# Ten head pairs' scores from scaled float16 halves, and more of the feed-forward's evacuations on ScalarE

## The chip, the cores and the metric

The kernel runs on one NeuronCore of a Trainium2 chip. The metric is the device time of one execution in microseconds (us); "before" is the median of three runs. Five engines work side by side: TensorE (PE), VectorE (DVE), ScalarE (ACT), GpSimd (POOL) and SyncE (SP), which issues the transfers.

## What is computed

```python
scores = scale * q @ k.T                       # 4 batches x 8 heads, 576 x 576, depth 64
thresh = max(scores, axis=-1) - tau
scores = where(scores >= thresh, scores, -1e9)
attn   = softmax(scores)                       # sum + 1e-9 in the denominator
x = (attn @ v) as [2304 tokens, 512]
g = relu(x @ w_in) ** 2                        # 512 -> 2048
x = g @ w_out                                  # 2048 -> 512
logits = x @ phi                               # 32 slots: 8 experts x 4
d = softmax(logits, over tokens); slots = d.T @ x
slots = per expert: relu(slots @ w1) @ w2      # 512 -> 1024 -> 512
out = softmax(logits, over slots) @ slots
```

## The kernel before

**Order.** A planner inside the kernel (class `Plan`) places every operation. `add(kind, engine, cost, fn, deps, key, takes, ...)` registers one with a planned duration, a key (lower goes first) and the buffers that it takes; on each engine the planner starts the ready operation with the lowest key. The result is a fixed order on every engine, SP's queue included. The costs are the planner's; no time here comes from them.

**Attention.** A pair is two heads of one batch; there are 16 pairs in 20 jobs (the first four pairs are cut into two jobs each). A job walks over tiles of 128 queries: j = 0 to 3 hold 128 queries of each of the two heads, j = 4 is the mixed tile with the last 64 queries of both. A full job has five tiles, and the 20 jobs have 80. For each tile:

- `s_mm` on PE: scores in float32, line 555 for the 64 remaining keys of both heads at once, line 560 for 512 keys of one head (64 rows of the array each); the mixed tile has lines 549 and 552.
- `top` on DVE (line 576): the scores, scaled, into `u`, and their row minimum; `bound` on POOL (582); `expo` on ACT (588); `keep` on DVE (592): the mask and the row sum.
- then, for all but the first batch, `high` on ACT (610) and `low` on POOL (614) split the result into float16 halves `hl`; `dturn` lets a DMA transpose them (621, SP); `av_split` multiplies by v's halves in float16 (713, 718). Mixed tiles and the first batch transpose on PE (line 250) and multiply in float32 (705). `evac` on DVE writes the feed-forward's input `xp` (735).

v's halves are made by `split_v`: squares with a running sum (480), the sum over partitions on PE (486), a power of two from it on DVE (`power`, 274 to 278), the high half on ACT (514), the low half on DVE (518).

**Feed-forward.** A unit is 256 tokens; there are nine. Two of a batch can begin once its four pairs are done, and `rem` holds the remainders of all batches. A unit has 16 blocks of 12 float16 matmuls on PE (998, "FFN blocks" below); after each two, `relu` (1007) on ACT and `square` on ACT (1015), or on DVE (1013) where `m2 % 4` is in `SQD`. Then comes its post work: logits (813 to 826), eight groups of four transposes (250), an evacuation of each group, on ACT (910) or on DVE (912) where `j` is in `GKD`, and the sums over tokens (925). PE fills the gaps of the next batch's attention with these.

**Loads.** `raw64` is a set of eight 512 KB buffers: first for the weights' conversion, later for `w_pre`, loads of weights for the mixture at the end.

Of the kernel before, what the change touches and what calls it, by code (L numbers as in the profile page):

```python
# [9 lines left out]
F32 = mybir.dt.float32  # L10
# [131 lines left out]
def tile_kernel(  # L142
# [139 lines left out]
    def conv_ops():  # L282
# [124 lines left out]
        for n in range(RB):  # L407
            add("w_pre", "SP", 0.5, lambda: state["wr"](), stores, 300.0 + n, ["raw64"], dma=1.46)

    xp, ev_at, xs_op, att = {}, {}, {}, []  # L410

    def attn_ops():
# [27 lines left out]
        def prep(x):  # L440
# [10 lines left out]
            for nm in "kqv":  # L451
                def lraw(nm=nm):
                    if nm == "v":
                        t = raw[p, nm] = at.tile([128, 2, 4 * D], F32, tag=nm + "raw", name="raw", bufs=2)
                        nc.sync.dma_start(
                            out=t, in_=v[b, h0:h0 + 2, 0:512, :].rearrange("h (r j) d -> r h (j d)", j=4)
                        )
                        return
                    t = d[nm + "t"] = at.tile([128, SQ], F32, tag=nm + "t", name=nm + "t", bufs=QKB)
                    nc.sync.dma_start(out=t, in_=src[nm][b, n])  # L460
                ld[nm] = add("lraw", "SP", 0.6, lraw, [], k0 - (5 if nm != "v" else 2), [nm + ("raw" if nm == "v" else "t")],
                             dma=0.73 if nm == "v" else 0.95)
# [3 lines left out]
            split = any(by_dma(x, j // 2) for j in jobs[x][1] if j < 4)  # L466
            if split or 0 in jobs[x][1]:
                split_v(x, split)

        def split_v(x, split):  # L470
# [12 lines left out]
            def stats():  # L483
                d["ps"] = mm_tile()
                for i in range(2):
                    nc.tensor.matmul(
                        d["ps"][:, 0:1], ones.to_broadcast([128, 128]), d["mx"][:, i:i + 1], start=i == 0, stop=i == 1
                    )

            def scales():  # L490
                mx = d["mx"]
                e = mx[:, 4:5]
                nc.vector.tensor_scalar(e, d["ps"][:, 0:1], 2.0**-80, None, ALU.max)
                if n == 0:
# [24 lines left out]

            ab = add("v_abs", "ACT", 0.9, absum, [d["v_op"], d["vr_op"]], k0, ["mx", "vh"])  # L520
            st = add("v_sum", "PE", 0.4, stats, [ab], k0, ["mm"])
            sc = add("v_scale", "DVE", 0.9 if split else 0.3, scales, [st], k0, rel=[("mm", st)])
            if n == NP - 1:
# [7 lines left out]
            plan.release(d["vs_ready"], [("vraw", d["v_op"]), ("vbd", d["vr_op"])])  # L531

        def tiles(p):
            d = P[p]
            b, kk = jobs[p][0] // NP, jobs[p][0] % NP
            G = [dict() for _ in range(3)]
            s_ops, av_ops, m_ops = [], [], []

            def tile_ops(n, j):
# [5 lines left out]
                def s_mm():  # L545
                    s = ps.tile([128, 3, 512], F32, tag="s", name="s", bufs=1)
                    o["s"] = s.rearrange("p c s -> p (c s)")
                    if mixed:
# [9 lines left out]
                    for a in range(2):  # L558
                        i = slice(64 * a, 64 * a + 64)
                        nc.tensor.matmul(s[:, 2 * a], lt[i], d["kt"][i, 0:512], start=True, stop=True)  # L560

                first_g = "first" not in gd
                S_ = add("s", "PE", 1.4, s_mm, d["ready"], k, ["s"])
                s_ops.append(S_)
                heads = (0,) if mixed else (0, 1)
                ks = []
                for a in heads:
# [3 lines left out]
                    def top(a=a, c=c):  # L571
                        if "sm" not in gd:
# [3 lines left out]
                        nc.vector.tensor_scalar(  # L576
                            u, o["s"][:, s0:s0 + S], nscale, None, ALU.mult, ALU.min, accum_out=gd["sm"][:, c:c + 1]
                        )
# [16 lines left out]

                    X = add("top", "DVE", 0.89, top, [S_], k, ["u"] + (["sm"] if first_g and not a else []), [("s", S_)])
                    if first_g and not a:
                        gd["first"] = X
# [182 lines left out]
            for o in s_ops:  # L781
                plan.release(o, [("kt", d["k_op"]), ("qt", d["q_op"])])
            for o in av_ops:
# [9 lines left out]
    def ffn_ops(units):  # L793
# [158 lines left out]
        for n, u in enumerate(units):  # L952
# [7 lines left out]
            def xhi(kk, u=u, x=x, up=up):  # L960
                if kk == 0:
                    x["x"] = xr if u == "rem" else xp[u]
                    x["h"] = fx.tile([128, KC, NU], F16, tag="xh", name="xh", bufs=2)
                nc.vector.tensor_scalar(x["h"][:, kk, :], x["x"][:, kk, :], up, None, ALU.mult)

# [8 lines left out]
            for kk in range(KC):  # L974
                xd = xdeps[kk::KC] + (hs[-1:] if kk else prev.get("hs", [])[-1:] + [xs_op[B if u == "rem" else u[0]]])
                h = add("xhi", "DVE", 0.2, lambda f=xhi, kk=kk: f(kk), xd, HI, [] if kk else ["xh"])
                l = add("xlo", "DVE", 0.37, lambda f=xlo, kk=kk: f(kk), [h] + ls[:1],
# [335 lines left out]
```

## Time and profile before

| | |
|---|---|
| median of three runs | 679.88 us (678.04 to 680.73) |
| the profiled execution | 685.74 us |
| its span | 684.0 us |
| PE, DVE, ACT, POOL busy | 619.8, 471.6, 418.0, 253.6 us |
| mean granted clock of TensorE, of full speed | 0.947 |

The span is the time from the first to the last instruction of the profiled execution. A busy share is an average over stages, so the rows below cut the span.

### The profile page before, as it was taken

The page shows a single profiled execution, that of the slowest core. Times are in us where ns is not written, and L with a number is a line of the kernel's source. Part 1 is how long each engine was busy: PE and PEld are TensorE (multiplying, and loading weights), DVE is VectorE, ACT ScalarE, POOL GpSimd, SP SyncE. Part 2 cuts the span into 40 slices and gives each one's busy share as a digit, 9 for nine tenths or more (in the row PEclk, how much of TensorE's full clock was granted, in tenths as well). Part 3 has the DMA queues.
Part 4 walks back from the last instruction along what each step waited for, and adds up shares of the span by engine and source line. Part 5 has one row for each costly group of instructions (what it writes and reads, how often), then busy time and mean ns, then how long its engine had stood idle before and what let it go on. Part 6 is the DMA issues. An engine that isn't in the chain of part 4 may idle for free.

```text
span 684.0 us, 13526 instructions
## 1 busy us (share of the span) xinstructions
PE 619.8 (91%) x5054; PEld 421.2 (62%) x5054; DVE 471.6 (69%) x1284; ACT 418.0 (61%) x782; POOL 253.6 (37%) x316
## 2 busy tenths in 40 slices
PE   1875989999999999799999999989999999998883
PEld 0443566667776676567757676756776878773321
DVE  4888889967678978887887888878895232231503
ACT  6898976765475776667776667856663443440203
POOL 2765563326434454445654425544550000001000
PEclk9996779997799999999999999989999999999997
DMA  8965154536669475464655627455434940258977
GB/s 279 349 218 174 57 188 163 177 96 180 160 154 257 92 143 106 97 132 86 133 104 116 143 52 138 91 124 89 86 71 134 410 169 33 97 203 308 371 284 276
DMA packets 151281, 111.82 MB, mean 163 GB/s; under 512 B 118960, under 2 KB 124080, under 8 KB 151216
## 3 DMA queue, kind: packets, MB, share of 16 engines
q1 hardware_dynamic: 151216, 110.96, 58.1%
q8 instruction: 40, 0.66, 0.4%
q14 instruction: 25, 0.20, 0.1%
HBM read 73.72 MB, written 8.91 MB: 121 GB/s over the span
## 4 chain that ended last, share of the span: by engine, by line
PE 67%; DVE 14%; ACT 10%; DMA 4%; issue 3%; SPq 1%; POOL 0%; DVEq 0%; ACTq 0%
PE mm L998 26%; PE mm L250 9%; PE s L560 8%; PE po L713 4%; PE po L705 3%; DVE e L592 3%; ACT raw L309 3%; PE mm L925 3%; PE s L555 2%; PE mm L1135 2%; DVE u L576 2%; ACT e L588 2%; DMA w<-in_moe_w_dram 2%; PE s L549 2%; DVE xl L969 2%
## 5 line engine op out<-in xcount | busy, mean ns | idle before, releaser
L998 PEld LDWEIGHTS <-w 128*128 128x128 f16 x1728 | 167.9, 99 | 39.3 <-issue 19.4
L614 POOL TENSOR_TENSOR hl<-e,hl 128x576 f16<-128x576 f32 x96 | 126.3, 1328 | 105.0 <-ACT hl L610 91.4
L998 PE MATMUL mm<-xh,w 128*128 128x256 f16 x1152 | 151.1, 275 | 1.4 <-DVE gk L912 1.3
L592 DVE SCALAR_TENSOR_TENSOR e<-u,sm,e 128x576 f32<-128x576 f32 x144 | 127.1, 898 | 24.8 <-ACT e L588 19.1
L588 ACT ACTIVATE e<-u,sm 128x576 f32<-128x576 f32 x144 | 109.5, 769 | 51.2 <-DVE u L576 47.1
L576 DVE TENSOR_SCALAR_CACHE_REDUCE u<-s,nscale 128x576 f32<-128x576 f32 x144 | 114.8, 811 | 22.7 <-PE s L560 14.7
L582 POOL TENSOR_SCALAR sm<-sm,tau_p 128x1 f32<-128x1 f32 x144 | 63.0, 440 | 124.1 <-DVE u L576 111.2
L998 PE MATMUL mm<-xl,w 128*128 128x256 f16 x576 | 86.9, 274 | 0.0
L1007 ACT ACTIVATE gt<-mm,scl 128x512 f32<-128x512 f32 x72 | 49.1, 682 | 56.0 <-PE mm L998 55.8
L560 PE MATMUL s<-kt,qt 64*128 64x512 f32 x256 | 82.1, 722 | 0.0
L610 ACT ACTIVATE hl<-e 128x576 f16<-128x576 f32 x96 | 63.9, 676 | 19.7 <-DVE e L592 19.3
L555 PE MATMUL s<-kt,qt 128*128 128x128 f32 x128 | 30.0, 319 | 33.2 <-DMA qt<-in_q_dram 13.3
L555 PEld LDWEIGHTS s<-kt,qt 128*128 128x128 f32 x128 | 21.5, 210 | 39.0 <-issue 18.2
L309 ACT ACTIVATE raw<-raw 128x512 f16<-128x512 bf16 x32 | 41.8, 1354 | 5.1 <-DMA raw<-in_moe_w_in_dram 4.3
L250 PE MATMUL mm<-ident_r,e 128*128 128x128 f32 (+1 forms) x224 | 38.8, 311 | 4.7 <-DVE e L592 4.5
L1098 POOL MEMSET cv<- 128x512 f32 x4 | 1.9, 525 | 103.8 <-PE mm L925 103.8
L250 PE MATMUL mm<-ident_r,gt 128*128 128x128 f32 x288 | 39.9, 284 | 0.1
L250 PEld LDWEIGHTS mm<-ident_r,gt 128*128 128x128 f32 x288 | 32.6, 146 | 12.0 <-issue 9.7
L250 PEld LDWEIGHTS mm<-ident_r,e 128*128 128x128 f32 (+1 forms) x224 | 29.7, 161 | 16.5 <-DVE e L592 7.7
L657 ACT ACTIVATE pt<-mm 128x512 f32<-128x512 f32 x48 | 28.3, 601 | 17.3 <-PE mm L250 17.0
L1013 DVE SCALAR_TENSOR_TENSOR gt<-mm,scl,gt 128x512 f32<-128x512 f32 x18 | 13.5, 748 | 33.0 <-ACT gt L1007 32.8
L713 PE MATMUL po<-pt,vh 128*64 128x256 f16 x576 | 35.9, 274 | 0.0
(172 smaller groups left out, 940.2 us busy)
## 6 DMA issues: line engine op xcount, KB each, us to landing
w<-in_moe_w_dram SPq DMA_DIRECT2D x17, 1024.0 KB, 13.1
w<-in_moe_w_dram SPq DMA_DIRECT2D x26, 512.0 KB, 7.9
raw<-in_moe_w_in_dram SPq DMA_DIRECT2D x16, 511.8 KB, 6.8
raw<-in_moe_w_out_dram SPq DMA_DIRECT2D x16, 511.8 KB, 4.4
kt<-in_k_dram SPq DMA_DIRECT2D x20, 320.0 KB, 3.8
qt<-in_q_dram SPq DMA_DIRECT2D x20, 320.0 KB, 4.3
raw<-in_v_dram SPq DMA_DIRECT2D x20, 256.0 KB, 3.5
w_out<-cv SPq DMA_DIRECT2D x16, 256.0 KB, 4.2
```

The costliest lines, as they stand in the source:

```text
L250: nc.tensor.transpose(out_, in_, ident[:n, :n])
L309: nc.scalar.activation(x[:, :, 3].bitcast(F16), x[:, :, 2].bitcast(BF16), AF.Copy)
L555: nc.tensor.matmul(s[:, 1].rearrange("p (c s) -> p c s", s=64)[:, 0:8:7], lt, d["kt"][:, 512:SQ], start=True, stop=True)
L560: nc.tensor.matmul(s[:, 2 * a], lt[i], d["kt"][i, 0:512], start=True, stop=True)
L576: nc.vector.tensor_scalar(u, o["s"][:, s0:s0 + S], nscale, None, ALU.mult, ALU.min, accum_out=gd["sm"][:, c:c + 1])
L582: nc.gpsimd.tensor_scalar(sm[:, 4 + c:5 + c], sm[:, c:c + 1], tau_p, None, ALU.add)
L588: nc.scalar.activation(e, o["u", a], AF.Exp, scale=-1.0, bias=gd["sm"][:, c:c + 1])
L592: nc.vector.scalar_tensor_tensor(e, o["u", a], sm[:, 4 + c:5 + c], e, ALU.is_le, ALU.mult, accum_out=sm[:, 8 + c:9 + c])
L610: nc.scalar.activation(o["hl"][:, a * S:(a + 1) * S], o["e"][:, a * S:(a + 1) * S], AF.Copy)
L614: nc.gpsimd.tensor_tensor(o["hl"][:, (2 + a) * S:(3 + a) * S], o["e"][:, c], o["hl"][:, c], ALU.subtract)
L713: nc.tensor.matmul(po[64 * a:64 * a + 64, :n_], d["vh"][:, y, c0:c0 + D], gd["pt"][:, :, c + 5 * a + m, :], start=i == 0 and m == 0, stop= ...
L998: nc.tensor.matmul(o["h"][:, i * NU:(i + 1) * NU], a, c, start=n_ == 0, stop=n_ == len(terms) - 1)
```

## The change

Jobs 10 to 19 (`QF = 10`, the last ten pairs) no longer use q and k in float32. `lraw` loads them into `raw64`, `split_qk` sums their squares (ACT, PE), makes a power of two for each (DVE), the high halves (ACT) and the low halves (DVE), and six copies from SBUF to SBUF (SP) lay them out so that one matmul over 128 rows multiplies high and low half of q by the high half of k. `fine_mm` adds the high half of q times the low half of k: eight float16 matmuls a tile, four of 512 and four of 64 columns. `GKD` and `SQD` are empty: all squares and all evacuations of transposed groups run on ACT. v's two sums become one matmul of two columns with a reduce on DVE. `w_pre` has a later key. The `XHA` branch is not taken.

```diff
-    GKD = (1, 3)
-    SQD = (3,)
+    GKD = ()
+    SQD = ()
     LOD = (0, 4)
+    QF = 10
+    XHA = ()
+    QL = 16.0
+    LL = 16.0
...
-            add("w_pre", "SP", 0.5, lambda: state["wr"](), stores, 300.0 + n, ["raw64"], dma=1.46)
+            add("w_pre", "SP", 0.5, lambda: state["wr"](), stores, 1000.0 + n, ["raw64"], dma=1.46)
...
+                    if x < QF:
+                        t = d[nm + "t"] = at.tile([128, SQ], F32, tag=nm + "t", name=nm + "t", bufs=QKB)
+                    else:
+                        d[nm + "r"] = t = rows.tile([128, 2 * CW], F32, tag="raw64", name="raw64", bufs=RB)
+                        t = t[:, 0:SQ]
...
-                for i in range(2):
-                    nc.tensor.matmul(
-                        d["ps"][:, 0:1], ones.to_broadcast([128, 128]), d["mx"][:, i:i + 1], start=i == 0, stop=i == 1
-                    )
+                nc.tensor.matmul(d["ps"][:, 0:2], ones.to_broadcast([128, 128]), d["mx"][:, 0:2], start=True, stop=True)
...
+                nc.vector.tensor_reduce(e, d["ps"][:, 0:2], AX.X, ALU.add)
...
+        def split_qk(x):
...
+                nc.scalar.activation(
+                    d[nm + "h"].bitcast(BF16)[:, 1], d[nm + "r"][:, 0:SQ], AF.Square, accum_out=d["st"][:, 0, i:i + 1]
+                )
...
+                nc.tensor.matmul(d["pq"][:, 0:2], ones.to_broadcast([128, 128]), d["st"][:, 0], start=True, stop=True)
...
+                nc.vector.tensor_scalar(s2, d["pq"][:, 0:2], 2.0**-80, None, ALU.max)
+                power(s2, t, f, inv)
+                d["nscale"] = t[:, 0:1]
+                nc.vector.tensor_scalar(t[:, 0:1], inv[:, 0:1], inv[:, 1:2], nscale, ALU.mult, ALU.mult)
...
+                nc.scalar.activation(d[nm + "h"][:, 0], d[nm + "r"][:, 0:SQ], AF.Copy, scale=d["st"][:, 3, i:i + 1])
...
+                nc.vector.scalar_tensor_tensor(
+                    d[nm + "l"], d[nm + "r"][:, 0:SQ], d["st"][:, 3, i:i + 1], d[nm + "h"][:, 0], ALU.mult, ALU.subtract
+                )
...
+                if i == 0:
+                    nc.sync.dma_start(out=h[64:128, 1], in_=h[64:128, 0])
+                elif i == 1:
+                    nc.sync.dma_start(out=h[0:64, 1], in_=o[64:128])
+                else:
+                    nc.sync.dma_start(out=h[64:128, 0], in_=o[0:64])
...
+            st = add("q_sum", "PE", 0.25, stats, [qs], k0, ["mm"])
+            sc = add("q_scale", "DVE", 1.0, scales, [st], k0, rel=[("mm", st)])
+            d["ready"] = []
+            for nm in "qk":
+                h = add("q_hi", "ACT", 0.75, lambda nm=nm: high(nm), [sc], k0)
+                l = add("q_lo", "DVE", 0.9, lambda nm=nm: low(nm), [h], k0)
+                m0 = add("q_move", "SP", 0.5, lambda nm=nm: move(nm, 0), [h], k0, dma=0.35)
+                m1 = add("q_move", "SP", 0.5, lambda nm=nm: move(nm, 1), [l if nm == "q" else h], k0, dma=0.35)
+                m2 = add("q_move", "SP", 0.5, lambda nm=nm: move(nm, 2), [l, m0, m1], k0, dma=0.35)
+                d["ready"] += [l, m2]
...
+                def fine_mm(s):
...
+                    def mm(a, full, main):
+                        r = slice(0, 128) if full or not main else slice(64 * a, 64 * a + 64)
...
+                        nc.tensor.matmul(o0, d["qh"][r, a, q0], kk, start=full, stop=not full)
+
+                    if mixed:
+                        order = [(a, f, m) for f in (True, False) for m in (True, False) for a in range(2)]
+                    else:
+                        order = [
+                            (0, True, True), (0, True, False), (0, False, False), (1, True, False),
+                            (1, False, False), (1, True, True), (0, False, True), (1, False, True),
+                        ]
```

The new lines shift the numbers: 610 becomes 707, 621 becomes 718, 713 becomes 810, 718 becomes 815, 910 becomes 1012, 998 becomes 1103, 1007 becomes 1112, 1015 becomes 1120; all new score matmuls are line 646.

SP's queue in the middle of the third batch, one pair, before (`hl` to `pt` is the transposition, L460 the load of the next pair's k and q, L455 that of v):

```order
L460 DMA kt<-in_k_dram 128x640
L460 DMA qt<-in_q_dram 128x640
L621 DMA_TRANSPOSE pt<-hl 128x18x128
L455 DMA raw<-in_v_dram 128x2x256
L621 DMA_TRANSPOSE pt<-hl 128x18x128 x3
```

and after (L581, L583 and L585 are the first, second and third copy of q or k; `raw_3677` holds that pair's q, k's low half included in its own buffer):

```order
L468 DMA raw_4621<-in_k_dram 128x640
L468 DMA raw_4636<-in_q_dram 128x640
L581 DMA qt<-qt 64x640
L583 DMA qt<-raw_3677 64x640
L718 DMA_TRANSPOSE pt<-hl 128x18x128
L585 DMA qt<-raw_3677 64x640
L581 DMA kt<-kt 64x640
L583 DMA kt<-kt 64x640
L585 DMA kt<-kt 64x640
L459 DMA raw<-in_v_dram 128x2x256
L718 DMA_TRANSPOSE pt<-hl 128x18x128 x3
```

The copies stand between the transpositions, and the third of each operand behind the first two.

PE's order ahead of the mixed tile of the last pair, before (`rb` is a reciprocal's transposition, L998 an FFN block, of which four follow here):

```order
L250 MATMUL mm<-ident_r,rb 128x128 x2
L555 MATMUL s<-kt,qt 128x2x64
L560 MATMUL s<-kt,qt 128x512 x2
L998 LDWEIGHTS w_125
L998 MATMUL mm<-xh,w_125 128x256
```

and after (from the end of the last but one av to the mixed tile's scores; `gt`, `gk`, `dk` and `al` belong to the sixth unit's post work):

```order
L815 MATMUL po<-pt,vh 128x256
L254 MATMUL mm<-ident_r,dT 128x32 x2
L974 MATMUL mm<-al,stack_f 128x1
L254 MATMUL mm<-ident_r,gt 128x128 x4
L254 MATMUL mm<-ident_r,rb 128x128 x2
L496 MATMUL mm<-mx,ones 128x2
L1027 MATMUL mm<-gk,dk 32x512 x4
L646 LDWEIGHTS qt
L646 MATMUL s<-kt,qt 64x512
```

No FFN block is left between the last score tiles. Counted over PE's whole order, 98 of the 144 FFN blocks stand ahead of attention's last po matmul before and 103 after; the sixth unit's post work stands behind that matmul, but for its first step, before, and ahead of it after.

ACT's order from the fifth unit's post work on, before (`gk` is the evacuation of four transposed blocks):

```order
L890 ACTIVATE ce<-ce 128x64
L657 ACTIVATE pt<-mm 128x4x128
L655 ACTIVATE pt<-mm 64x128
L751 ACTIVATE rr<-mm 128x128
L588 ACTIVATE e<-u,sm 128x576
L610 ACTIVATE hl<-e 128x576
L588 ACTIVATE e<-u,sm 128x576
L910 ACTIVATE gk<-mm 128x512
L610 ACTIVATE hl<-e 128x576
```

and after:

```order
L992 ACTIVATE ce<-ce 128x64
L1012 ACTIVATE gk<-mm 128x512
L684 ACTIVATE e<-u,sm 128x576 x2
L848 ACTIVATE rr<-mm 128x256
L1012 ACTIVATE gk<-mm 128x512
L523 ACTIVATE vh<-raw,mx 128x512
L523 ACTIVATE vh<-vbd_128,mx 128x128
L707 ACTIVATE hl<-e 128x576
L684 ACTIVATE e<-u,sm 128x576
L707 ACTIVATE hl<-e 128x576
L1112 ACTIVATE gt<-mm,scl 128x512
L1012 ACTIVATE gk<-mm 128x512
```

The evacuations that stood on DVE stand between the exponentials and the copies of attention.

## Rows read from the trace of the kernel before

**Rows 1.** The page: span, and busy time, share and instructions of each engine.
```profile
span 684.0 us, 13526 instructions
...
PE 619.8 (91%) x5054; PEld 421.2 (62%) x5054; DVE 471.6 (69%) x1284; ACT 418.0 (61%) x782; POOL 253.6 (37%) x316
```

**Rows 2.** Stretches: length; PE, PEld, DVE, ACT, POOL busy; clock; DMA share; GB/s.
```profile
200.00:520.00 320.00, 308.58 (x2788) 216.63 (x2787) 265.32 (x743) 218.16 (x420) 154.12 (x197) 0.98 0.55 114
520.00:616.00 96.00, 94.79 (x889) 75.09 (x889) 29.88 (x75) 38.22 (x69) 0.00 (x0) 1.00 0.48 181
```

**Rows 3.** Waits from 200 to 520 us: total, times, longest.
```profile
PE s L555 <- DVE u L576: 6.0, 4, 2.8
...
DVE e L592 <- ACT e L588: 10.0, 11, 2.8
...
ACT e L588 <- DVE u L576: 39.6, 33, 3.1
```

**Rows 4.** TensorE in order of time: start, length, line, out<-in, shapes.
```profile
355.30 1.02 PE L549 MATMUL s<-kt,qt 128*128 128x512 f32 x2
...
356.42 1.48 PE L713 MATMUL po<-pt,vh 128*64 128x256 f16 x24
357.83 0.50 PE L718 MATMUL po<-pt,vh 128*128 128x256 f16 x3
358.17 0.39 PE L555 MATMUL s<-kt,qt 128*128 128x128 f32 x2
...
359.54 1.06 PE L925 MATMUL mm<-gk,dk 128*32 128x512 f32 x8
```

**Rows 5.** The chain that ended last, around the end of attention.
```profile
523.64 0.49 DVE xp L735
...
527.14 17.15 PE mm L998 x156
```

**Rows 6.** VectorE in order of time: two steps of `power`, and v's low half.
```profile
286.90 0.15 DVE L275 TENSOR_SCALAR mx<-mx 128x1 int32<-128x1 int32 x1
287.09 0.15 DVE L276 TENSOR_SCALAR mx<-mx 128x1 int32<-128x1 int32 x1
...
288.44 0.73 DVE L518 SCALAR_TENSOR_TENSOR vh<-raw,mx,vh 128x512 f16<-128x512 f32 x1
289.09 0.48 DVE L518 SCALAR_TENSOR_TENSOR vh<-vbd,mx,vh 128x128 f16<-128x128 f32 x1
```

**Rows 7.** Groups by line and form, VectorE, 200 to 520 us: busy, mean ns.
```profile
L912 DVE COPY gk<-mm 128x512 f32<-128x512 f32 x22 | 14.9, 683 | 1.5 <-PE mm L250 1.5
...
L1013 DVE SCALAR_TENSOR_TENSOR gt<-mm,scl,gt 128x512 f32<-128x512 f32 x11 | 8.2, 748 | 3.4 <-ACT gt L1007 3.3
```

**Rows 8.** ScalarE in order of time: a scaled copy, Square with accumulator.
```profile
346.20 0.72 ACT L514 ACTIVATE vh<-raw,mx 128x512 f16<-128x512 f32 x1 [0.22 <-DVE mx L277]
346.82 0.39 ACT L514 ACTIVATE vh<-vbd,mx 128x128 f16<-128x128 f32 x1
...
371.16 0.63 ACT L480 ACTIVATE vh<-raw 128x512 bf16<-128x512 f32 x1 [0.22 <-PE po L718]
...
371.79 0.29 ACT L481 ACTIVATE vh<-vbd 128x128 bf16<-128x128 f32 x1
```

**Rows 9.** Groups by line and form, ScalarE, 200 to 520 us: busy, mean ns.
```profile
L1015 ACT ACTIVATE gt<-gt 128x512 f32<-128x512 f32 x34 | 21.1, 622 | 0.3
...
L910 ACT ACTIVATE gk<-mm 128x512 f32<-128x512 f32 x22 | 12.7, 590 | 4.0 <-PE mm L250 3.9
```

**Rows 10.** Waits of SP's queue from 200 to 520 us: total, times, longest.
```profile
SPq L621 <- POOL sm L582: 148.2, 32, 9.5
```

**Rows 11.** Two more stretches, columns as in rows 2.
```profile
80.00:120.00 40.00, 36.77 (x261) 25.88 (x259) 37.13 (x97) 30.41 (x53) 21.10 (x24) 0.87 0.45 152
442.00:460.00 18.00, 15.31 (x133) 9.36 (x132) 14.13 (x40) 9.89 (x21) 8.68 (x10) 0.85 0.48 103
```

**Rows 12.** The 64 KB loads of v's remainders (line 449): issue to landing.
```profile
DMA to landing us min/median/max: 2.4/5.0/10.0
```

More of the change, by code (lines that the diff above doesn't have):

```diff
@@ L458, in lraw @@
                         return
-                    t = d[nm + "t"] = at.tile([128, SQ], F32, tag=nm + "t", name=nm + "t", bufs=QKB)
+                    if x < QF:
[3 more added lines that the diff above has]
+                        t = t[:, 0:SQ]
                     nc.sync.dma_start(out=t, in_=src[nm][b, n])
-                ld[nm] = add("lraw", "SP", 0.6, lraw, [], k0 - (5 if nm != "v" else 2), [nm + ("raw" if nm == "v" else "t")],
+                tag = "vraw" if nm == "v" else nm + "t" if x < QF else "raw64"
+                ld[nm] = add("lraw", "SP", 0.6, lraw, [], k0 - (2 if nm == "v" else 5 if x < QF else LL), [tag],
                              dma=0.73 if nm == "v" else 0.95)
@@ L466, in prep @@
             split = any(by_dma(x, j // 2) for j in jobs[x][1] if j < 4)
+            if x >= QF:
+                split_qk(x)
             if split or 0 in jobs[x][1]:
@@ L520, in split_v @@
             ab = add("v_abs", "ACT", 0.9, absum, [d["v_op"], d["vr_op"]], k0, ["mx", "vh"])
-            st = add("v_sum", "PE", 0.4, stats, [ab], k0, ["mm"])
-            sc = add("v_scale", "DVE", 0.9 if split else 0.3, scales, [st], k0, rel=[("mm", st)])
+            st = add("v_sum", "PE", 0.25, stats, [ab], k0, ["mm"])
+            sc = add("v_scale", "DVE", 1.0 if split else 0.4, scales, [st], k0, rel=[("mm", st)])
             if n == NP - 1:
@@ L547, in s_mm @@
                     o["s"] = s.rearrange("p c s -> p (c s)")
+                    if p >= QF:
+                        fine_mm(s)
+                        return
                     if mixed:
@@ L560, in s_mm @@
                         nc.tensor.matmul(s[:, 2 * a], lt[i], d["kt"][i, 0:512], start=True, stop=True)
+                def fine_mm(s):
+                    kl = d["kl"]
+                    def mm(a, full, main):
+                        r = slice(0, 128) if full or not main else slice(64 * a, 64 * a + 64)
+                        h = slice(64 * a, 64 * a + 64) if mixed else slice(0, 128)
+                        c = 512 + 64 * a
+                        q0 = slice(c, c + 64) if mixed else slice(j * 128, j * 128 + 128)
+                        k0 = slice(0, 512) if main else slice(c, c + 64)
+                        o0 = s[h, 0 if mixed else 2 * a] if main else s[h, 1, 0:64] if mixed or not a else s[h, 1, 448:512]
+                        kk = d["kh"][r, a, k0] if full else kl[r, k0]
+                        nc.tensor.matmul(o0, d["qh"][r, a, q0], kk, start=full, stop=not full)
[6 more added lines that the diff above has]
+                        ]
+                    for y in order:
+                        mm(*y)
                 first_g = "first" not in gd
-                S_ = add("s", "PE", 1.4, s_mm, d["ready"], k, ["s"])
+                S_ = add("s", "PE", (0.6 if mixed else 0.9) if p >= QF else 1.4, s_mm, d["ready"], k, ["s"])
                 s_ops.append(S_)
@@ L781, in tiles @@
             for o in s_ops:
-                plan.release(o, [("kt", d["k_op"]), ("qt", d["q_op"])])
+                if p < QF:
+                    plan.release(o, [("kt", d["k_op"]), ("qt", d["q_op"])])
+                else:
+                    plan.release(o, [("kt", d["kt_op"]), ("qt", d["qt_op"])])
+            for o in t_ops if p >= QF else ():
+                plan.release(o, [("raw64", d["k_op"])])
             for o in av_ops:
@@ L963, in xhi @@
                     x["h"] = fx.tile([128, KC, NU], F16, tag="xh", name="xh", bufs=2)
-                nc.vector.tensor_scalar(x["h"][:, kk, :], x["x"][:, kk, :], up, None, ALU.mult)
+                if kk in XHA:
+                    nc.scalar.activation(x["h"][:, kk, :], x["x"][:, kk, :], AF.Copy, scale=up)
+                else:
+                    nc.vector.tensor_scalar(x["h"][:, kk, :], x["x"][:, kk, :], up, None, ALU.mult)
             def xlo(kk, x=x, up=up):
@@ L975, in ffn_ops @@
                 xd = xdeps[kk::KC] + (hs[-1:] if kk else prev.get("hs", [])[-1:] + [xs_op[B if u == "rem" else u[0]]])
-                h = add("xhi", "DVE", 0.2, lambda f=xhi, kk=kk: f(kk), xd, HI, [] if kk else ["xh"])
+                h = add("xhi", "ACT" if kk in XHA else "DVE", 0.45 if kk in XHA else 0.2, lambda f=xhi, kk=kk: f(kk), xd, HI, [] if kk else ["xh"])
                 l = add("xlo", "DVE", 0.37, lambda f=xlo, kk=kk: f(kk), [h] + ls[:1],
```

30 lines of the change are left out of this document (27 added, 3 removed).

## The prediction

> **What bounds the kernel now.** I read the engines' totals first. TensorE (PE) is busy 619.8 us of the 684.0 us span, VectorE (DVE) 471.6, ScalarE (ACT) 418.0 [rows 1]. An average over stages decides nothing, so I cut the span at the places where the work changes. From 200 to 520 us attention of the ten affected pairs runs with the feed-forward of earlier batches between; PE is busy 308.58 of 320 us (96.4%), DVE 265.32 (83%), ACT 218.16 (68%). Attention's last evacuation starts at 523.64 us [rows 5]; from there to 616 us only feed-forward is left, and from 520 to 616 PE is busy 94.79 of 96 us [rows 2]. The mixture of experts comes behind that and is left as it was. So PE sets the pace in these two stages, and a microsecond of PE work taken out is a microsecond of time as long as PE doesn't wait in its place. It already does so now and then: its longest wait in the stage is for DVE's `top` (u L576), 6.0 us in four waits [rows 3]. The profiled execution took 685.74 us; the median of the runs is 679.88. I make the sum against 685.74 and subtract the difference from 679.88.
>
> **Scores: what PE gains.** A float32 tile starts at 358.17 us with the remainder matmul and ends when the next work starts at 359.54: 1.37 us. A mixed tile takes from 355.30 to 356.42: 1.12 us [rows 4]. The new tile has eight float16 matmuls. For their price the nearest row is the feed-forward's float16 block: 156 matmuls of 256 columns in 17.15 us, 0.110 us each [rows 5]. So 512 columns are 0.22 us, and the last two of a tile lie in different row halves of the array and run side by side, as the 24 of po L713 do: 1.41 us until po L718 starts is 0.118 us for each pair of 256 columns [rows 4]. That is 3 x 0.22 = 0.66 us. The four of 64 columns are in no row. Below: a quarter of 0.110, 0.027 each. Above: 0.113, the pace of po L718, three matmuls in 0.34 us, each with its own full weight load [rows 4], since each of the four loads 128 weights too. The tile is then 0.77 to 1.11 us; I take the middle, 0.94. The Trainium skill, "TensorE: Matmul & The Clock Gate", Back-to-back issue gap, gives about 60 cycles, 25 ns, for 1 to 64 columns, or 62 ns where decoding binds; by that the tile would be 0.76 or 0.91 us, an estimate from that page, and no run here shows it. The mixed tile is two pairs of 512 and two pairs of 64 columns: 0.50 to 0.68, taken 0.59. Forty tiles save 0.43 each (0.26 to 0.60), ten mixed ones 0.53 (0.44 to 0.62): 17.2 + 5.3 = 22.5 us (15 to 30). `q_sum` adds ten matmuls like v_sum's, and v_sum loses one of its two, sixteen in all: taken as nothing. **PE: -22 us.**
>
> **What DVE pays.** Each pair adds seven operations on 128x2, pitched at 0.19 us like those of `power` [rows 6], and one reduce of that size: 1.5 us. `q_lo` is a scalar_tensor_tensor with 640 columns. Its 512-column like starts 0.65 us ahead of the next [rows 6]; by columns the pitch is 0.65 x 640/512 = 0.81, so 1.6 for two. Ten pairs: +31 us. Gone are 22 evacuations (683 ns) and 11 squares (748 ns) of this stage [rows 7], 14.9 + 8.2 = 23 us, or 20.5 by their pitch, 0.08 less each. Net **+10.5 us**: 276 of the stage's time.
>
> **What ACT pays.** Squares for q and k: the 512-column Square with its accumulator read holds ACT 0.63 us until the next starts; by columns 0.79 for 640. The scaled copy holds it 0.62 us at 512 columns [rows 8]; 0.78. Four of them are 3.1 us a pair, 31 us in all. The 22 moved evacuations cost 590 ns each, the 11 squares 622 [rows 9], 17.5 us by pitch. **+48 us**, 266 in the stage. ACT here copies a block out of PSUM faster than DVE does, 590 against 683 ns [rows 7, 9]. [...]
>
> **Other parts at nothing.** Loads: the same bytes into other buffers. The `w_pre` loads keep their place ahead of the end of attention and have until 616 us. In the last unit eight evacuations stand on ACT alone: 0 to +1 us, taken 0. Six copies of 80 KB a pair join SP's queue; they are needed only when the next pair begins. What covers them: SP waits 148.2 us in 32 waits for GpSimd ahead of the transposes of the stage, 4.6 each [rows 10]. A late transposition delays `hl`, then `high`, then av. Without cover they cost what rival 3 says.
>
> **Where the order puts the gain.** Ahead of attention's last po stand 98 of 144 blocks now, 103 after, and also the post work of the sixth unit. So five blocks (6.6 us by 1.32 us each) and one unit's post leave the stage after 520 us. A post takes, from the 92.4 us between 523.6 and 616 less 46 blocks (60.7 us), 31.7 us for some 3.7 posts, 8.5 us. If attention ends where it did, the gain is 15 us. The stage from 200 us on then holds 308.6 - 22 + 15 = 302 us of PE work, to be done beside 276 of DVE and 266 of ACT. At today's share (96.4%) it takes 313 us, 7 less than the 320: gain 22. The nearest row for crowded engines is 80 to 120 us: DVE 37.13 of 40 us (93%), ACT 76%, and PE 36.77, 92% [rows 11]. At 92% the stage takes 328 us: gain 7. The new shares, DVE 86% and ACT 83%, lie between: I take 93.7%, 322 us, gain 13. **Sum: 685.7 - 22 (PE) + 9 (more waits) = 672.7 us, 13 below the profiled execution; 667 us beside the median.** Its own range is 661 to 673.
>
> **Rivals.**
> 1. *The whole gain is kept* (chance 0.17). PE's waits don't grow, 96.4% holds: 680 - 22, and with the low price of the 64-column matmuls 680 - 30: 650 to 660. For it: DVE and ACT stay below 87%, and the waits on DVE were few [rows 3]. Against: feed-forward runs out earlier; the last score tiles have only post work between them.
> 2. *ACT and DVE take the bound* (0.20). The shares are summed over 320 us, but evacuations and squares come in bursts ahead of attention's exp. ACT's exp waited 39.6 us for DVE and DVE's `keep` 10.0 us for ACT [rows 3]: the two work in turn on one chain, and each new operation lengthens a turn. With PE at 90% the stage takes 335.5 us and the gain is gone: 674 to 683, middle 678. Where PE waits, the clock suffers as well: from 442 to 460 us PE was busy 15.31 of 18 us and was granted 0.85 of 2.4 GHz, that is partly its 1.2 GHz level [rows 11]. [...]
> 3. *SP's queue: slower* (0.15). Each pair's third copy waits on SP until the first two have landed, and behind it stand the transposes. A 64 KB load landed in 2.4 to 10.0 us, median 5.0 [rows 12]. Up to 4.6 us is cover. Each microsecond beyond it, once a pair, costs 10 us; the point from which it decides is 4.6 + 2.2 = 6.8 us. At 7.8: 680 - 22 + 32 = 690. For it: the copies share the queues with transposes. Against: the median is below the cover.
>
> **How the numbers follow.** The forecast has 0.48, the rivals 0.17, 0.20 and 0.15. A measurement tells 0.5%, 3.4 us, from no change. Faster: 0.48 + 0.17, and 0.05 of rival 2 that ends below 676.5, 0.70. Within: 0.14. Slower: rival 3 and 0.01 of rival 2, 0.16. For eight in ten the range leaves out the low end of rival 1 (below 655, 0.07) and most of rival 3 (above 682, 0.13): 655 to 682.
>
> **What the profile after would show.** The score matmuls' line at about 0.94 us a tile (0.59 mixed), PE's total near 598 us. In the affected stage DVE near 86% and ACT near 83%, PE near 94%. Attention's last evacuation at 522 to 528 us, the stage from there to the tail some 78 us in place of 92. SP's waits at the third copy under 5 us, and no wait of a score tile for a copy. Wrong would be: a tile above 1.1 us (the weight loads bind), PE below 91% with exp or `keep` as releaser (rival 2), or po waiting for pt (rival 3).

## The result and the profile after

The changed kernel takes 684.25 us (median of 20 runs), the kernel before 679.54 in the runs beside it: ratio 1.0072, 95% interval 1.0048 to 1.0096. It is slower by 5 us where 13 less were forecast. The profiled execution took 682.69 us. Its totals, which answer to [rows 1], from the page of the kernel after:

```profile
span 680.9 us, 14000 instructions
PE 604.4 (89%) x5142; PEld 413.8 (61%) x5142; DVE 477.3 (70%) x1336; ACT 470.0 (69%) x896; POOL 267.3 (39%) x316
```

PE's busy time fell by 15 us, to 604.4 (forecast near 598), and the span by 3. The windows of the kernel after (first line: the stretch of [rows 2]; then attention's end, and two places at which PE waited) have busy time and count for PE, PEld, DVE, ACT and POOL, then the granted clock, the DMA share and GB/s. The last line is of the kernel before, profiled a second time, in the first stretch:

```profile
200.00:520.00 320.00, 297.88 (x2871) 211.72 (x2870) 276.65 (x794) 252.66 (x500) 161.34 (x192) 0.96 0.62 126
520.00:614.00 94.00, 93.05 (x873) 74.11 (x869) 14.86 (x54) 47.57 (x87) 0.22 (x1) 1.00 0.53 199
505.00:515.00 10.00, 4.75 (x41) 2.25 (x38) 9.19 (x22) 3.80 (x8) 3.55 (x5) 0.93 0.43 99
515.00:520.00 5.00, 4.73 (x32) 3.63 (x34) 3.47 (x10) 1.52 (x5) 2.54 (x2) 0.50 0.28 52
...
265.00:270.00 5.00, 4.23 (x56) 2.28 (x48) 4.90 (x16) 2.35 (x8) 1.35 (x2) 1.00 0.63 117
270.00:280.00 10.00, 9.39 (x65) 7.11 (x66) 9.66 (x31) 7.39 (x17) 3.95 (x5) 0.66 0.19 43
```

```profile
200.00:520.00 320.00, 308.45 (x2830) 217.16 (x2830) 265.88 (x742) 215.13 (x415) 152.51 (x195) 0.99 0.56 115
```

PE is busy 93.1% of the stage (forecast 93.7) and DVE 276.65 us (forecast 276). But the granted clock is 0.96 where it was 0.98 in [rows 2] and 0.99 in the second profile, and a busy share counts slow matmuls as busy. The rows of after show where it fell: from 505 to 515 us PE is busy 4.75 of 10, and then gets 0.50, its 1.2 GHz level; around 270 us it works with gaps, and then gets 0.66.

**An account for each kernel.** I split a span into PE's idle time, the loss to the lower level, (1 - mean clock) x span, and the rest: PE's work as if at the full level. For the loss it counts the lower level as if PE had worked all through it, so it is a rough figure. The mean clock after is:

```profile
core 0: 680.9 us, clock 0.937
```

| kernel | median | span | PE work | loss | idle |
|---|---|---|---|---|---|
| before, the profile shown | 679.5 | 684.0 | 583.5 | 36.3 | 64.2 |
| before, profiled again (clock 0.957) | 678.6 | 676.8 | 582.0 | 29.1 | 65.7 |
| after | 684.25 | 680.9 | 561.5 | 42.9 | 76.5 |

The execution that [rows 1] show is one of that kernel's slow ones: it took 685.74 us, and of the 74 runs of before that were timed beside the experiments all but one took less, so the second profile is the one to compare with. Against it, work fell by 20.5 us (forecast 22), idle time grew by 10.8 (forecast 9) and the loss by 13.8 (forecast: nothing). Against the profile shown the three are 22.0, 12.3 and 6.6, mostly since its own loss is 7.2 above that of the second. The loss of one kernel differs much between executions (20 to 42 us over those 74 runs), so I also take medians: the mean clock is 0.953 over the 74 runs of before, a loss of 32 us, and 0.9365 over the 20 of after, 43 us.

**The tiles** (timeline of PE, kernel after: start, duration, what; consecutive matmuls of one shape stand in one row). First an ordinary tile, then a mixed one:

```profile
308.54 0.41 PE L646 MATMUL s<-kt,qt 128*128 128x512 f16 x2
308.78 0.19 PE L646 MATMUL s<-raw,qt 128*128 128x64 f16 x1
308.81 0.19 PE L646 MATMUL s<-kt,qt 128*128 128x64 f16 x1
308.84 0.19 PE L646 MATMUL s<-raw,qt 128*128 128x64 f16 x1
308.87 0.38 PE L646 MATMUL s<-kt,qt 128*128 128x512 f16 x1
309.18 0.39 PE L646 MATMUL s<-raw,qt 64*128 64x512 f16 x2
309.50 0.30 PE L810 MATMUL po<-pt,vh 128*64 128x256 f16 x2
...
320.68 0.44 PE L646 MATMUL s<-kt,qt 128*64 128x512 f16 x4
321.05 0.55 PE L646 MATMUL s<-raw,qt 64*64 64x512 f16 x4
321.53 0.64 PE L915 MATMUL mm<-gt,wphi 128*32 128x256 f32 x8
```

From 308.54 to 309.50 is 0.96 us (forecast 0.94); the 64-column matmuls start 0.03 us apart, the low bound. The mixed tile takes 0.85, not 0.59 (321.53 less 320.68).

**What DVE pays** (groups of the kernel after: busy time, mean ns of one):

```profile
L574 DVE SCALAR_TENSOR_TENSOR raw<-raw,kt 128x640 f16<-128x640 f32 x10 | 10.8, 1085 | 0.0
L574 DVE SCALAR_TENSOR_TENSOR raw<-raw,raw,qt 128x640 f16<-128x640 f32 x10 | 9.8, 978 | 0.6 <-DMA raw<-in_k_dram 0.6
L278 DVE TENSOR_SCALAR raw<-raw 128x2 int32<-128x2 int32 x10 | 4.8, 480 | 0.3
L279 DVE TENSOR_SCALAR raw<-raw 128x2 int32<-128x2 int32 x10 | 4.0, 396 | 0.3
L280 DVE TENSOR_SCALAR raw<-raw 128x2 int32<-128x2 int32 x10 | 2.8, 278 | 0.3
L566 DVE TENSOR_SCALAR raw<-raw,nscale 128x1 f32<-128x1 f32 x10 | 2.7, 273 | 0.4
L281 DVE TENSOR_SCALAR raw<-raw 128x2 int32<-128x2 int32 x10 | 2.7, 269 | 0.3
L282 DVE TENSOR_SCALAR raw<-raw 128x2 int32<-128x2 int32 x10 | 1.6, 162 | 0.0
L563 DVE TENSOR_SCALAR raw<-mm 128x2 f32<-128x2 f32 x10 | 1.6, 157 | 1.0 <-PE mm L559 0.8
```

The seven small operations sum to 20.2 us and `q_lo` to 20.6: 41 us where the forecast had 29.3 for them. The timelines of DVE and, last, POOL show why the means are so far above 0.19:

```profile
336.35 0.15 DVE L563 TENSOR_SCALAR raw<-mm 128x2 f32<-128x2 f32 x1
336.54 0.31 DVE L278 TENSOR_SCALAR raw<-raw 128x2 int32<-128x2 int32 x1
336.89 1.20 DVE L279 TENSOR_SCALAR raw<-raw 128x2 int32<-128x2 int32 x1
338.12 0.23 DVE L280 TENSOR_SCALAR raw<-raw 128x2 int32<-128x2 int32 x1
...
335.00 3.06 POOL L711 TENSOR_TENSOR hl<-e,hl 128x576 f16<-128x576 f32 x2 [4.98 <-ACT hl L707]
```

L279 takes 1.20 us and ends at 338.09, three hundredths after GpSimd's `low` ends at 338.06.

**Waits** of the stage from 200 to 520 us (us in total, times, longest), a wait of PE in its timeline, and pieces of the chain that ended last (start, duration), all of the kernel after:

```profile
PE s L646 <- DVE u L672: 8.0, 6, 2.3
PE mm L254 <- POOL rb L781: 5.1, 1, 5.1
...
495.33 0.42 PE L646 MATMUL s<-kt,qt 128*128 128x512 f16 x2 [2.25 <-DVE u L672]
```

```profile
SPq L581 <- ACT qt L570: 26.0, 6, 6.1
...
SPq L585 <- DMA kt<-kt: 3.4, 3, 1.5
```

```profile
506.49 1.95 DVE vh L527 x2
508.44 1.42 DVE xl L1074
509.86 0.26 DVE xh L1069
510.12 0.60 DVE sg L1036
510.71 0.40 DVE xl L1074
511.11 1.48 DVE e L688 x4
512.59 0.74 DVE u L672 x2
```

SP's third copy (L585) waited 3.4 us in all for the first two, and PE shows no wait for a copy or for `pt`: rival 3 didn't come, though SP waited 26.0 us for the high halves (L570) ahead of the first copies. Ahead of that `rb` the chain is DVE without a break, late work of v, of the feed-forward and of the tiles, and PE waits 5.1 us there. With the 2.25 us ahead of the last full score tile that is 7.4 of the stage's 22.1 us of idle time, and no FFN block stands in PE's order between 483 and 516 us. Attention's last evacuation starts at 530.57 us, forecast 522 to 528 (523.64 in [rows 5], 516.6 in the second profile). From there to 614 us, where only the mixture is left, are 83 us, forecast 78.

### The profile page after: what moved, and what is told of

Read it like the earlier page. It is cut to its first block, busy times and chain, and to the rows that moved or that the text cites. A ratio compares the mean times of both kernels' runs of the same rounds, so it can differ in the third digit from the quotient of the medians.

```text
span 680.9 us, 14000 instructions
## 1 busy us (share of the span) xinstructions
PE 604.4 (89%) x5142; PEld 413.8 (61%) x5142; DVE 477.3 (70%) x1336; ACT 470.0 (69%) x896; POOL 267.3 (39%) x316
## 4 chain that ended last, share of the span: by engine, by line
PE 60%; DVE 18%; ACT 10%; issue 5%; DMA 3%; SPq 1%; DVEq 0%; ACTq 0%
PE mm L1103 24%; PE mm L254 9%; PE s L646 5%; DVE e L688 5%; PE po L810 4%; PE s L633 3%; DVE u L672 3%; ACT raw L313 2%; PE mm L1240 2%; PE po L802 2%; PE mm L1027 2%; ACT e L684 2%; DMA w<-in_moe_w_dram 2%; DVE xl L1074 2%; PE mm L915 1%
## 5 line engine op out<-in xcount | busy, mean ns | idle before, releaser
L711 POOL TENSOR_TENSOR hl<-e,hl 128x576 f16<-128x576 f32 x96 | 131.2, 1382 | 80.2 <-ACT hl L707 58.2
L688 DVE SCALAR_TENSOR_TENSOR e<-u,sm,e 128x576 f32<-128x576 f32 x144 | 129.7, 912 | 13.2 <-ACT e L684 12.5
L678 POOL TENSOR_SCALAR sm<-sm,tau_p 128x1 f32<-128x1 f32 x144 | 70.1, 489 | 133.8 <-DVE u L672 108.2
L672 DVE TENSOR_SCALAR_CACHE_REDUCE u<-s,raw 128x576 f32<-128x576 f32 x90 | 72.0, 809 | 16.7 <-PE s L646 16.5
L1120 ACT ACTIVATE gt<-gt 128x512 f32<-128x512 f32 x72 | 45.0, 625 | 1.1
L672 DVE TENSOR_SCALAR_CACHE_REDUCE u<-s,nscale 128x576 f32<-128x576 f32 x54 | 43.0, 809 | 3.2 <-PE s L625 1.6
L646 PEld LDWEIGHTS <-qt 128*128 128x128 f16 (+3 forms) x400 | 22.1, 100 | 34.0 <-issue 24.1
L646 PE MATMUL s<-kt,qt 128*128 128x512 f16 (+1 forms) x200 | 33.9, 294 | 8.0 <-DVE u L672 8.0
L254 PEld LDWEIGHTS mm<-ident_r,gt 128*128 128x128 f32 x288 | 33.2, 148 | 11.0 <-issue 7.3
L1012 ACT ACTIVATE gk<-mm 128x512 f32<-128x512 f32 x68 | 36.5, 591 | 4.7 <-PE mm L254 4.3
```

The costliest lines, as they stand in the source:

```text
L254: nc.tensor.transpose(out_, in_, ident[:n, :n])
L646: nc.tensor.matmul(o0, d["qh"][r, a, q0], kk, start=full, stop=not full)
L672: nc.vector.tensor_scalar(u, o["s"][:, s0:s0 + S], d.get("nscale", nscale), None, ALU.mult, ALU.min, accum_out=gd["sm"][:, c:c + 1])
L678: nc.gpsimd.tensor_scalar(sm[:, 4 + c:5 + c], sm[:, c:c + 1], tau_p, None, ALU.add)
L688: nc.vector.scalar_tensor_tensor(e, o["u", a], sm[:, 4 + c:5 + c], e, ALU.is_le, ALU.mult, accum_out=sm[:, 8 + c:9 + c])
L711: nc.gpsimd.tensor_tensor(o["hl"][:, (2 + a) * S:(3 + a) * S], o["e"][:, c], o["hl"][:, c], ALU.subtract)
```

## The experiments

Theory 1: the scale's work on DVE takes the gain, with ACT's squares as its other half. Theory 2: the move to ACT costs. The Trainium skill, "ScalarE: Activation LUTs", Rules for kernel authors, puts relu, max, min, add and multiply on VectorE; of the moved work that names the squares, and not the copies out of PSUM. Theory 3: each version gets another order of instructions from the planner, and that order is what differs. Ratios are to the kernel before on the same chip, with 95% intervals; the account of every kernel, each from one profiled execution, stands at the end.

**Before, again.**

> The kernel before, unchanged, for a second profile. If the profile shown before was an unusual execution, this one lies near 679.5 us, its mean granted clock above 0.947 and its PE busy time below 619.8 us, and then part of the miss is the baseline. If the profile was usual, clock and busy time come out as they were within 0.003 and 3 us.

678.58 us, in the table above.

**The parts alone.** The first is the change with no pair split, the second the change with the move taken out:

```diff
-    QF = 10                     # e1
+    QF = 20
-    GKD = ()                    # e2
-    SQD = ()
+    GKD = (1, 3)
+    SQD = (3,)
```

> All scores in float32 (no pair split), squares and evacuations all on ScalarE. Theory 1 (the split's new work on VectorE and ScalarE takes the gain): VectorE is relieved by some 20 us in the stage, so the time is that of the kernel before or less, 672 to 681 us. Theory 2 (the move to ScalarE costs): 683 us or more. Theory 3 (the re-planned order itself shifts the time by some us either way, whatever is changed): anything from 674 to 688, without relation to the load.

> Scores split for the ten pairs, squares and evacuations shared between VectorE and ScalarE as before the change. Theory 1: VectorE carries the split's 31 us on top of the old load, 300 of 320 us, and the time rises above that of the change, 688 to 698 us. Theory 2: without the move the gain on PE shows, 665 to 675 us. Theory 3: 676 to 690.

689.24 us, 1.0155 (1.0097 to 1.0213), and 708.7 us, 1.0436 (1.0383 to 1.0489). Each is worse than both together, so the parts don't add up: something besides their work differs.

**The scale's work taken out, with the order that follows.** e3 multiplies by 1 and leaves out squares, sum and scale; e4 makes the squares and doesn't use them; e5 leaves out the squares and makes the scale from a constant:

```diff
-            ks = add("q_sq", "ACT", 0.9, lambda: sums("k"), ...)     # e3, e5
-            st = add("q_sum", "PE", 0.25, stats, [qs], k0, ["mm"])   # e3, e4
-            sc = add("q_scale", "DVE", 1.0, scales, ...)             # e3, e4
```

> The change with q and k split at a constant scale of 1: the squares on ScalarE (16 us), the sum on PE and the seven small VectorE operations a pair (13 us) are left out, the halves, copies and matmuls stay. Theory 1: a good part of PE's gain comes back, 668 to 677 us. Theory 2: little changes, 681 to 685 us. Theory 3: anything from 674 to 688.

> As the constant scale, but the squares of q and k stay on ScalarE (their sums go unused); the sum on PE and the small VectorE operations are left out. If ScalarE's 16 us are what the constant scale won, this lies near the change, 680 to 685 us. If VectorE's small operations and the wait for them are, it stays near the constant scale, 664 to 670 us.

> As the constant scale, but the sum on PE and the seven VectorE operations a pair stay (they work on a constant); the squares on ScalarE are left out. If VectorE's operations are the cost, 678 to 684 us. If ScalarE's squares are, 664 to 670 us. If both add up, half way, 672 to 678 us.

664.22 us (0.9779, 0.9731 to 0.9828), 669.37 (0.9858, 0.9800 to 0.9915) and 672.2 (0.9921, 0.9888 to 0.9955). Without the scale, and in the order that follows, the kernel is 20 us faster. The squares add 5 to that, the chain 8, and both 20: again more than the sum.

**A shorter scale, and other planned costs.** e6 takes sums of absolute values and a reciprocal (a scale that is no power of two), three operations in place of seven, planned at 0.5, so its order differs too; e7 only tells the planner the costs of the forecast (one of its three lines is shown):

```diff
-                nc.vector.tensor_scalar(s2, d["pq"][:, 0:2], 2.0**-80, None, ALU.max)      # e6
-                power(s2, t, f, inv)
+                nc.vector.tensor_scalar(inv, d["pq"][:, 0:2], 2.0**-40, 2.0**-18, ALU.max, ALU.mult)
+                nc.vector.reciprocal(f, inv)
-            sc = add("q_scale", "DVE", 1.0, ...)                                           # e7
+            sc = add("q_scale", "DVE", 1.33, ...)
```

> The change with three VectorE operations in place of seven for the scale of a pair (a reciprocal of the mean magnitude in place of a power of two; the sums on ScalarE stay): four fewer in the chain, 40 in all, some 8 us of VectorE. Theory 1, VectorE's part of it: 674 to 680 us. If ScalarE is the cost: 681 to 685 us.

> The change with the same instructions, and only three planned durations of the split set nearer to the trace (0.79, 1.33 and 0.81 us in place of 0.9, 1.0 and 0.9), so that the planner writes another order. Theory 3 (the order itself moves the time by some us): a time more than 3 us away from 684. Theories 1 and 2: 681 to 687 us.

673.31 us (0.9916, 0.9889 to 0.9943) and 686.15 (1.0104, 1.0047 to 1.0161).

**The move alone, and the rest alone.** e8 is before with empty `GKD` and `SQD`. e9 is the change without split and move: left are `w_pre`'s later key and v's sums by one matmul.

```diff
-            add("w_pre", "SP", 0.5, lambda: state["wr"](), stores, 300.0 + n, ...)
+            add("w_pre", "SP", 0.5, lambda: state["wr"](), stores, 1000.0 + n, ...)
```

> The kernel before with one edit alone: all squares and block evacuations of the feed-forward on ScalarE, and the places of the scores, loads and sums as they were. If the move itself costs (the Trainium skill's rule on ScalarE), it is slower by 5 to 12 us, as the run with the move and all the rest but the split was (+9.4 us). If what cost there was the rest of the change (later w_pre loads, one matmul for v's sums, the order that follows), it is within 3 us of the kernel before. TensorE's work stays near 582 us at full clock either way; VectorE falls by about 22 us, ScalarE rises by some 19.

> The change without the split and without the move: left are the later w_pre loads and v's sums by one matmul and a reduce. By themselves they should cost nothing: within 3 us of the kernel before. If they or the order that follows from them are what made the run with the move slower, this one is slower by 5 to 10 us too, with fewer feed-forward blocks ahead of the last tile.

683.31 us (1.0039, 0.9995 to 1.0083) and 670.95 us (0.9873, 0.9806 to 0.9939). By e8 the move, planned anew, makes no difference that can be told. The second I had not expected: the part that I had put at nothing is 8 us faster.

**Two tries at a faster version.** e10 is e6 with sums over every fourth column (planned at 0.5 each), which rests the scale on a quarter of the data; e11 is e6 with `QF = 8`.

> The version with sums of absolute values and a reciprocal, but each sum over every fourth column (160 of 640), so ScalarE has about 0.4 us less for each of the twenty sums, 8 to 10 us in all, and everything else stays. If ScalarE's load is part of what is lost, 668 to 671 us; if only VectorE's chain and TensorE's clock count, 673 as that version took.

> The version with sums of absolute values and a reciprocal, with twelve pairs split in place of ten. If TensorE still sets the pace, two more pairs save 2 x 2.1 = 4 us: 669. If VectorE and ScalarE set it, the two pairs cost what they load on these engines and give nothing: 673 to 677.

666.02 us (0.9791, 0.9738 to 0.9844), the fastest of those that make a scale from their data; and 702.57 (1.0316, 1.0236 to 1.0396), which neither of its two forecasts gave.

**The order kept, the work changed.** The planner places an operation by its planned cost and engine, and calls its function there. So a function can be changed while every instruction keeps its place. e12 to e14 do that with the change; their scale is the constant 1, or (e13) from a tenth of the columns. In e15 (order of e9) and e17 (order of e2) all evacuations and squares are planned as they were, some on DVE, and issued on ACT. e16 is before, its order kept, with v's sums by one matmul.

```diff
-                power(s2, t, f, inv)                                    # e12, e14
+                nc.vector.tensor_scalar(d["st"][:, 3], d["pq"][:, 0:2], 0.0, 1.0, ALU.mult, ALU.add)
-                    ... d[nm + "r"][:, 0:SQ], AF.Square, ...            # e13, e14
+                    ... d[nm + "r"][:, 0:64], AF.Square, ...
-                        if j not in GKD:                                # e15, e17
+                        if j not in ():
```

> The change with every instruction where its order has it, but the scale of a pair made by one VectorE operation on 128x2 (which writes the constant 1) in place of seven; the squares and the sum on TensorE stay, their value isn't used. If the chain of seven small operations is a cost of its own, 674 to 678 us (6 to 10 less than the change); if the differences seen so far came from other orders of the instructions, it stays at 684.

> The change with every instruction where its order has it, but each sum of squares over 64 columns in place of 640, so ScalarE is free some 0.6 us earlier in each of twenty, 12 us in all; the scale comes out another. If ScalarE's load counts, 676 to 680 us; if VectorE's chain alone counts, 683 to 685.

> The change with its order kept, squares over 64 columns and one operation in place of seven, with the constant 1 as scale: both edits of the two runs beside it. If the scale's work is what took the gain, it comes near the 664 us of the version with a constant scale and no squares at all: 664 to 670. If the order of the instructions was a good part of that run's gain, 674 to 680.

> The kernel without the split and with the rest of the change (671 us with its evacuations and squares shared as before), in the same order on TensorE, but all block evacuations and squares issued on ScalarE at the places that they had. If the move costs by ScalarE's load, it is slower by 8 to 18 us, as the version was that was planned with them on ScalarE (689). If that was its order (80 blocks of the feed-forward ahead of the last tile in place of 92), it stays within 4 us of 671.

> The kernel before with v's sums by one matmul of two columns and a reduce on VectorE in place of two matmuls, and every other instruction where it was. The 64 matmuls on 128x1 took TensorE 10.4 us; half of them gone is 4 to 5 us of its work. If TensorE sets the pace, 674 to 676 us; if it is hidden, 679.

> The split with the rest of the change in the order that it got with evacuations and squares shared between the engines (708.7 us), but all of these issued on ScalarE at the places that they had. If VectorE's load was what made that version slow, 684 to 690 us, as the change; if the order made it slow, above 700.

| kernel | median | ratio (95%) | PE work | loss | idle |
|---|---|---|---|---|---|
| e1 no split | 689.24 | 1.0155 | 576.5 | 35.1 | 76.3 |
| e2 no move | 708.7 | 1.0436 | 561.0 | 53.1 | 93.4 |
| e3 no scale | 664.22 | 0.9779 | 558.7 | 31.1 | 72.2 |
| e4 squares, no chain | 669.37 | 0.9858 | 555.7 | 38.0 | 73.5 |
| e5 chain, no squares | 672.2 | 0.9921 | 564.4 | 28.8 | 77.0 |
| e6 reciprocal | 673.31 | 0.9916 | 558.0 | 40.4 | 75.5 |
| e7 planned costs | 686.15 | 1.0104 | 555.4 | 45.1 | 83.3 |
| e8 move alone | 683.31 | 1.0039 | 582.6 | 34.1 | 65.9 |
| e9 rest alone | 670.95 | 0.9873 | 577.3 | 23.3 | 66.0 |
| e10 sampled | 666.02 | 0.9791 | 557.0 | 35.2 | 71.3 |
| e11 twelve pairs | 702.57 | 1.0316 | 560.7 | 47.9 | 86.0 |
| e12 chain cut | 674.98 | 0.9938 (0.9904 to 0.9972) | 561.8 | 43.2 | 69.5 |
| e13 squares cut | 684.82 | 1.0116 (1.0071 to 1.0161) | 562.2 | 40.3 | 81.1 |
| e14 both cut | 676.08 | 0.9979 (0.9956 to 1.0003) | 560.2 | 36.3 | 74.9 |
| e15 e9, moved | 669.5 | 0.9893 (0.9852 to 0.9933) | 579.4 | 25.4 | 62.9 |
| e16 one matmul | 678.71 | 0.9978 (0.9940 to 1.0015) | 578.4 | 33.2 | 66.8 |
| e17 e2, moved | 699.07 | 1.0267 (1.0200 to 1.0334) | 555.5 | 49.4 | 90.8 |

In the same order, cutting the chain gives 9 us (684.25 to 674.98): sixty instructions and 15.6 us of DVE less, and 7.0 us less idle time of PE (4.8 of it from the 25th score tile to attention's last av). The totals of e12:

```profile
span 674.5 us, 13941 instructions
PE 605.0 (90%) x5142; PEld 415.5 (62%) x5142; DVE 461.7 (68%) x1276; ACT 470.1 (70%) x896; POOL 266.9 (40%) x316
```

Cutting the squares gives nothing, alone or with the chain. After's two long waits at attention's end stay in e14, as long as they were (in e12 they are 2.24 and 3.59), so cutting the scale's work doesn't remove them. PE's timeline in e14:

```profile
486.43 0.66 PE L643 MATMUL s<-kt,qt 128*128 128x512 f16 x2 [2.25 <-DVE u L669]
505.12 0.69 PE L254 MATMUL mm<-ident_r,rb 128*128 128x128 f32 x2 [5.13 <-POOL rb L778]
```

e16 has v's sums by one matmul and gains nothing that can be told, so e9's 8 us come from `w_pre`'s key or from the order that follows it; which of the two isn't shown.

And the move in the same order: e9's totals, then e15's.

```profile
span 666.6 us, 13473 instructions
PE 600.6 (90%) x5022; PEld 407.9 (61%) x5022; DVE 473.8 (71%) x1300; ACT 419.7 (63%) x782; POOL 257.9 (39%) x316
```

```profile
span 667.7 us, 13478 instructions
PE 604.8 (91%) x5022; PEld 410.2 (61%) x5022; DVE 441.9 (66%) x1246; ACT 446.6 (67%) x836; POOL 260.3 (39%) x316
```

32 us of DVE become 27 of ACT and the time stays (670.95 to 669.5). e1 has e15's instructions on the same engines, in the order that the planner makes when it knows of the move, and takes 20 us more: ahead of its last score tile stand 80 FFN blocks, ahead of e15's 92. So what e1 showed was its order. e17 against e2 is the same move with the split: 10 us less; and after against e17, the same instructions on the same engines in another order, another 15.

## Why the prediction was wrong

The step that failed is the sum, "685.7 - 22 (PE) + 9 (more waits) = 672.7". It turns PE's busy share into time as if the clock stayed what it was: the share came as forecast (93.1% for 93.7), but a part of it was at the lower level. The clock I had named under rival 2 with [rows 11] and given no term. Against the second profile the terms are -20.5 (work, forecast -22), +10.8 (idle time, forecast +9) and +13.8 (clock, forecast 0): 4 us more in place of 13 less. The medians say the same, 11 us more loss. So what the clock took is about as much as the whole gain that was forecast. Against the profile shown the clock's part looks smaller, 6.6, and 7.4 us of the miss seem to lie in "subtract the difference from 679.88": that execution lay 5.9 us above the median, with 7.2 us more loss than the second, an excess and not a constant to carry over, and the profiled execution of after lies 1.6 below its own median.

- **Scores, nearly right in sum.** The ordinary tile came at 0.96 (0.94): forty save 0.41 each. The mixed one came at 0.85 (0.59): ten save 0.27 each, not 0.53. That is 19.1 us for 22.5. v's sums and `q_sum`, put at nothing together, gave 1 us more: v's 64 matmuls took 10.4 us in a profile of before and its 32 take 6.2 after, but `q_sum`'s twenty take 3.1. e16, v's part alone, shows 3.6 us less work, and no time that can be told.
- **DVE, mis-sized.** "Each pair adds seven operations on 128x2, pitched at 0.19 us": 20.2 us in place of 13.3. `q_lo`: 20.6 in place of 16. The price of 0.19 came from 128x1 rows [rows 6], which GpSimd doesn't hold up. The stage's total still came at 276 us, as forecast, and that is luck: its other work between 200 and 520 us was less by as much, as attention now ends later.
- **The chain's place.** I priced it by DVE's share of the stage. It has a cost by itself, as rival 2 said of turns on one chain: 9 us in e12, 0.9 a pair. Rival 2 was the nearest (674 to 683), and it named the clock; but its share of 90% for PE didn't come, and ACT's squares are no part of it: cutting them in the same order gave nothing (e13), with ACT at 79% of the stage.
- **The move to ScalarE.** It costs nothing in the same order (e15), and with the split it gives 10 us (e17); [rows 7, 9] said so, 590 ns for a copy in place of 683 and 622 for a square in place of 748. For the squares this speaks against the rule of the Trainium skill named with theory 2.
- **The order.** I counted blocks ahead of attention's end and took the rest as given. The runs show that one set of instructions takes 15 to 20 us more or less by its order (e1 and e15, e17 and after). Telling the planner the forecast's costs (e7) gave none of it back. So part of e3's and e10's distance to after is order too: with the order kept, e14 has squares over a tenth of the columns and a chain of one operation, and takes 676; e3, with neither and an order of its own, 664.
- **Where the scores' gain went.** e15 takes 669.5 us, e14 676.1. e14 has 19 us less work on PE and pays it back as 12.0 of idle time and 10.9 of loss. Of the idle time 7.4 us are the two waits at attention's end; e15's longest wait between 200 and 520 us is 1.7. What remains of the split in e14 is `q_lo`, the scaled halves, the copies and the order. No run leaves out the copies or `q_lo`, so which of these makes PE wait stays open, and so does which displaced operation costs the 15 to 20 us of a poor order.

## What to carry to other kernels

Where an engine at 95% gets less work, its own price is the easy half: list what each new operation stands behind on the other engines, and give the clock after each new wait a term in the sum. Take a profile's own excess (here 7 us of loss to the lower clock level) for an accident until a second profile shows it again: read against the first profile alone, the clock seemed to cost half of what it did. Where a planner sets the order, first run the change's work in the old order and the old work in the new one; here the order alone moved the time by more than the whole gain that was forecast.

## What the runs showed of the hardware

- **GpSimd holds up a small operation of DVE.** In the trace of after ten of the fifty 128x2 integer operations of lines 278 to 282 overlap GpSimd's `low` (L711); they take 0.89 us on average, the other forty 0.17. Of the 105 on 128x1, nineteen overlap it, and all take 0.15 to 0.16. The Trainium skill has it in "SBUF — State Buffer", section "SBUF: two separate sides": an operation of VectorE that uses both its read ports, or has two inputs in SBUF, and one of GpSimd take a shared port pair in turn, for a whole instruction. The trace agrees, and `q_lo`, which has two inputs in SBUF, fits too: the eight beside `low` took 1.26 us, the other twelve 0.88. By these rows the chain written as two on 128x1 would be fourteen operations of some 0.15 us that `low` doesn't hold up, an estimate; no run here tried it.
- **Four float16 matmuls of 64 columns start 0.03 us apart**, each with a weight load of its own, where [rows 4] have 0.113 for full loads that follow matmuls of 256 columns.
- **The granted clock fell behind waits of PE, though not behind every one.** Between 186 and 520 us of after six stretches of 3 to 7 us got 0.50 to 0.52, the 1.2 GHz level, with PE busy in nearly all of each. Ahead of them PE had waited 1.67, 1.76, 1.22, 1.93, 2.25 and 5.15 us. In the two profiles of before PE waits 2.8 us for `u` (L576) at the same matmul; behind it the clock fell in one and not in the other. Two stretches of after, then the one of before that [rows 1] show, then the second profile of before:

```profile
439.00:445.00 6.00, 6.00 (x24) 2.76 (x23) 3.75 (x17) 3.88 (x9) 0.85 (x2) 0.50 0.53 98
497.00:500.00 3.00, 3.00 (x25) 1.97 (x21) 2.31 (x6) 1.33 (x3) 3.00 (x2) 0.51 0.93 173
```

```profile
284.00:287.00 3.00, 3.00 (x16) 2.15 (x13) 2.04 (x8) 1.64 (x6) 1.85 (x2) 0.51 0.13 27
```

```profile
279.00:290.00 11.00, 10.97 (x86) 7.47 (x89) 10.23 (x30) 8.20 (x17) 5.61 (x7) 1.00 0.50 97
```
